# One tiling of the TensorE array throughout, the output product in one step, a band spread from one product, and another written-out order

## The chip, the cores and the metric

The kernel runs on one core of one Trainium2 chip. The metric is the time of the device in microseconds for one execution; of several runs the median is told.

## The reference

A causal convolution of seven taps, whose weights are a softmax over the taps for each of eight heads, and then a token mixer without a softmax. With B = 8, S = 4224, D = 192, H = 8 heads of 24 columns, KC = 7 taps and a hidden width DH = 64:

```python
w = softmax(weight, axis=-1)                     # [8, 7], with 1e-9 added to the sum
y[b, s, h, :] = sum_k w[h, k] * x_padded[b, s + k, h, :]    # six zero rows ahead of x
wq, wk = y @ w_q, y @ w_k                        # [B, S, 64]
W = (wq @ wk^T) / 8                              # [B, S, S]
mixed = W @ y
out = maximum(mixed, 0) @ w_out                  # float32
```

The S x S matrix is never formed: `mixed = wq @ (wk^T y) / 8`, and `wk^T y = w_k^T (y^T y)`, so that the mixer needs the Gram matrix `y^T y` (192 x 192) of a batch.

## The kernel before

**Tiling.** A batch's sequence is cut into 35 chunks of 122 tokens, each with six rows of the chunk before (`XW`, 128 partitions, cast to bf16 by the load). For what follows the transposition, it is cut into superblocks: four of 1024 tokens (two halves of 512, `nh` = 2) and one of 128 (`nh` = 1). The 192 columns of D are split as 128 (LO) and 64 (HI).

**Stages of a batch,** all on TensorE, each followed by an evacuation from PSUM on ScalarE (ACT) or VectorE (DVE):
- `conv` (L559): for each pair of heads, a product with a band matrix (`BAND`, 128 x 128 for each head), over nine (batch 0) or 18 chunks; evacuated to `Y` (L578).
- `tr_lo` (L598) and `tr_hi` (L633): transposes of the chunks' 128 and 64 columns, evacuated to `YTL` (L605) and `YTH` (L640). `tr_hi` writes two chunks to the two halves of the partitions.
- `wq` (L658, L662): the products with `w_q`, two halves of the superblock on the two halves of the array's columns; evacuated to `WQT` (L678).
- `gram` (L694): the Gram matrix, six chunks a step, three matmuls a chunk with 64 stationary columns each, in a PSUM bank of its own.
- `turn` (L720) and `m` (L737): from the Gram matrix the mixing weights `MSB` (64 rows twice, for the two halves) and `MBD` (two 64 x 64 blocks on the diagonal), evacuated on ACT (L755).
- `mix_lo` (L784) and `mix_hi` (L795) of the batch before: with `nh` = 2, `mix_lo` is two matmuls of 64 rows each, one on each half of the array's rows; then the maximum with zero to `RT` (L807 on ACT, L808 on DVE).
- the output product, two token groups of 128 in each half at a time: `fin_hi` (L835, 64 rows, on the halves of the array's rows) and `fin_lo` (L853, 128 rows), evacuated to `OUT` (L869) and stored by SP (L877).

So the array is used in four shapes (rows x columns): 128x128, 128x64 (two column halves), 64x128 (two row halves) and 64x64.

**Order.** Every operation is an `Op` with an estimate of its length. `Planner.plan` places them one by one: on each engine the operation with the lowest `vt` among those that its estimates call ready. An operation on TensorE with another shape (`mode`) than the last one pays `STAY` on its `vt` and `SWITCH` on its start. Operations for `both` go to the engine of ACT and DVE that is free first. PSUM has seven banks for this. What comes out is a fixed order for each engine, with semaphore waits. The `vt` of an operation is a formula of batch and position, plus `TURN[kind]`.

**Start.** The weights of the convolution come by one load (L338). `IDENT` is made by DVE and POOL (L345, L359). The softmax is a chain on DVE and ACT (L375 to L391). The band is made in two halves of four heads: for each tap one product on DVE (L412, `IDENTW` shifted times the tap's weight), summed on TensorE (L423) and copied by ACT (L433); the products lie in `OUT`. `conv` waits for its heads' half (`band_done`). The loads of `x` are issued on POOL (L479), in four groups for batch 0 and two for each later batch. `w_q`, `w_k` and `w_out` come by nine loads on SP (L503), issued when batch 0's third group has landed, with one semaphore; ten casts on ACT (L508) follow, and `wq`, `m` and the output product each wait for all of them.

## Time and profile before

| | |
|---|---|
| median of 3 runs | 177.99 us (177.98 to 179.53) |
| the profiled execution | 178.53 us |
| its span | 176.8 us |
| TensorE busy | 161.5 us, 2454 matmuls |
| DVE, ACT, POOL busy | 123.5, 122.6, 30.3 us |
| granted TensorE clock | 0.993 of full speed on average |

The span is the time from the first to the last instruction in the trace of one execution. PE is TensorE's matmuls and PEld its weight loads, which overlap with matmuls. In rows of the timeline the columns are start, duration, engine, line, operation, output and inputs, shape (stationary rows*columns, then the moving operand) and count; a merged row's duration is from the first start to the last end, and a matmul's own duration holds some 0.2 us of latency beside its streaming. In a row by stretches of time come the length, the busy time and number of instructions of the engine, the granted clock, the DMA share and GB/s.

### The profile page before, as it was taken

To read this page: it belongs to the slowest core of one execution; us is meant where nothing else is said; L and a number is where in the kernel's file an instruction comes from. 1 tells how busy PE (TensorE), PEld (TensorE's weight loads), DVE (VectorE), ACT (ScalarE), POOL (GpSimd) and SP (SyncE) were. 2 spreads that over 40 slices of the span, in tenths; PEclk is the share of its full clock that TensorE was granted. 3 is DMA by queue.
4 is the path that set the end of the run, shared out by engine and by line. 5 is a ranking of instruction groups with operands and counts; after the bars stand their busy time and mean duration, and the time that the engine had idled before them with its cause. 6 is when DMAs were issued, how large, how long until landed. Compare 5 with 4: busy or idle time off the path is not lost.

```text
span 176.8 us, 5567 instructions
## 1 busy us (share of the span) xinstructions
PE 161.5 (91%) x2454; PEld 112.3 (64%) x2454; DVE 123.5 (70%) x219; ACT 122.6 (69%) x209; POOL 30.3 (17%) x39
## 2 busy tenths in 40 slices
PE   0589849999999999999999999999999999999880
PEld 0249737676766777767686577666775778666440
DVE  5948776887567477677969866797658775887660
ACT  4054364957789996797768767587779846968870
POOL 7999731525230000000000000000000000000000
PEclk9999999999999999999999999999999999999997
DMA  3999999999999999999999995530844075556697
GB/s 30 160 190 189 197 197 190 190 194 191 212 318 312 249 230 333 248 307 232 286 283 233 322 266 203 231 151 4 352 185 180 28 296 226 233 237 279 257 398 287
DMA packets 48151, 40.26 MB, mean 228 GB/s; under 512 B 37632, under 2 KB 40960, under 8 KB 48128
## 3 DMA queue, kind: packets, MB, share of 16 engines
q0 software_dynamic: 36128, 13.61, 64.7%
q1 hardware_dynamic: 12000, 26.31, 39.9%
q8 instruction: 19, 0.31, 0.7%
q14 instruction: 4, 0.03, 0.0%
HBM read 27.56 MB, written 25.95 MB: 303 GB/s over the span
## 4 chain that ended last, share of the span: by engine, by line
PE 81%; DMA 8%; ACT 3%; SPq 2%; POOL 2%; issue 1%; POOLq 0%
PE ps L853 15%; PE ps L694 14%; PE ps L559 11%; PE ps L835 9%; PE ps L598 7%; DMA xw<-in_x_dram 5%; PE ps L633 5%; PE ps L784 5%; PE ps L658 5%; PE ps L795 5%; PE ps L662 4%; DMA whi<-in_moe_w_out_dram 3%; SPq L503 2%; POOL xw L479 1%; ACT out_sb L869 1%
## 5 line engine op out<-in xcount | busy, mean ns | idle before, releaser
L869 DVE COPY out_sb<-ps 128x768 f32<-128x768 f32 (+1 forms) x36 | 32.0, 891 | 25.4 <-PE ps L853 25.3
L807 ACT ACTIVATE rt<-ps 128x1024 bf16<-128x1024 f32 (+3 forms) x50 | 37.9, 770 | 14.0 <-PE ps L784 13.4
L578 ACT CAST y<-ps 122x864 bf16<-122x864 f32 (+3 forms) x49 | 36.9, 793 | 8.1 <-PE ps L559 7.6
L869 ACT COPY out_sb<-ps 128x768 f32<-128x768 f32 (+1 forms) x36 | 26.6, 746 | 10.7 <-PE ps L853 10.2
L694 PE MATMUL ps<-y 122*64 122x128 bf16 (+2 forms) x840 | 34.0, 222 | 0.0
L479 POOL DMA_DIRECT2D xw<-in_x_dram x34 | 29.9, 908 | 19.4 <-issue 18.6
L694 PEld LDWEIGHTS ps<-y 122*64 122x64 bf16 x840 | 28.0, 110 | 8.1 <-issue 7.6
L559 PE MATMUL ps<-xw,band 128*128 128x432 bf16 (+3 forms) x144 | 31.4, 323 | 0.8 <-ACT band L433 0.7
L853 PE MATMUL ps<-wol,rt 128*128 128x192 bf16 x264 | 30.5, 250 | 0.0
L853 PEld LDWEIGHTS ps<-wol,rt 128*128 128x128 bf16 x264 | 21.0, 116 | 7.8 <-issue 2.9
L578 DVE CAST y<-ps 122x816 bf16<-122x816 f32 (+3 forms) x23 | 20.6, 912 | 3.9 <-PE ps L559 3.6
L605 DVE COPY ytl<-ps 128x976 bf16<-128x976 bf16 (+1 forms) x40 | 23.0, 589 | 0.6 <-PE ps L598 0.2
L808 DVE TENSOR_SCALAR rt<-ps 128x512 bf16<-128x512 f32 (+3 forms) x30 | 20.1, 681 | 4.7 <-PE ps L784 2.7
L598 PE MATMUL ps<-ident,y 122*128 122x122 bf16 x280 | 20.5, 216 | 0.4 <-DVE y L578 0.4
L835 PE MATMUL ps<-woh,rt 64*128 64x192 bf16 x264 | 20.0, 250 | 1.0 <-ACT rt L807 0.7
L598 PEld LDWEIGHTS ps<-ident,y 122*128 122x128 bf16 x280 | 17.5, 97 | 4.4 <-ACT y L578 0.6
L640 DVE COPY yth<-ps 128x512 bf16<-128x512 bf16 (+1 forms) x40 | 14.9, 378 | 5.5 <-PE ps L633 5.1
L633 PE MATMUL ps<-ident,y 122*64 122x122 bf16 (+1 forms) x344 | 17.0, 217 | 0.0
L559 PEld LDWEIGHTS ps<-xw,band 128*128 128x128 bf16 x144 | 11.4, 97 | 7.8 <-issue 2.2
L658 PE MATMUL ps<-ytl,wql 128*64 128x512 bf16 (+1 forms) x72 | 14.6, 368 | 1.9 <-ACT woh L508 1.9
L835 PEld LDWEIGHTS ps<-woh,rt 64*128 64x128 bf16 x264 | 11.3, 114 | 7.9 <-ACT rt L807 1.5
L678 ACT CAST wqt<-ps 128x512 bf16<-128x512 f32 (+1 forms) x24 | 12.4, 532 | 5.2 <-PE ps L662 4.7
(63 smaller groups left out, 128.0 us busy)
## 6 DMA issues: line engine op xcount, KB each, us to landing
out_dram<-out_sb SPq DMA_DIRECT2D x28, 768.0 KB, 5.0
xw<-in_x_dram POOLq DMA_DIRECT2D x7, 816.0 KB, 30.3
xw<-in_x_dram POOLq DMA_DIRECT2D x7, 768.0 KB, 35.6
out_dram<-out_sb SPq DMA_DIRECT2D x8, 384.0 KB, 3.1
xw<-in_x_dram POOLq DMA_DIRECT2D x2, 432.0 KB, 8.3
out_dram<-out_sb SPq DMA_DIRECT2D x8, 96.0 KB, 3.6
xw<-in_x_dram POOLq DMA_DIRECT2D x1, 384.0 KB, 5.1
xw<-in_x_dram POOLq DMA_DIRECT2D x8, 45.8 KB, 23.8
```

Source lines behind the costliest of these rows:

```text
L479: lambda e, op, part=part: e.dma_start(*part),
L559: last = e.matmul(PS[:, o : o + n * GRP], BAND[:, h, :], XW[:, b, c0 : c0 + n, GRP * h : GRP * h + GRP], start=True, stop=True,)
L578: return e.copy(dst, src) if op.engine == "ACT" else e.tensor_copy(dst, src)
L598: last = e.transpose(ps[:, o : o + w], Y[0:w, yb, c, 0:LO], IDENT[0:w, 0:w])
L605: lambda e, op: e.tensor_copy(YTL[:, t0:t1], bank(mm_l.bank).bitcast(BF16)[:, 0:cols]),
L633: last = e.transpose(ps[64 * i : 64 * i + HI, o : o + w], Y[0:w, yb, c, LO:D], IDENT[0:w, 0:w])
L658: last = e.matmul(ps[64 * i : 64 * i + DH, 0:n], WQL[:, :], YTL[:, t0 + i * n : t0 + (i + 1) * n], start=True, stop=False)
L694: mm = e.matmul(bank(GB)[p : p + 64, o : o + z - r], Y[0:w, yb, c, r : r + 64], Y[0:w, yb, c, r:z], start=st, stop=end, skip_group_check=True,
L807: return e.activation(dst, src(), AF.Relu)
L835: last = e.matmul(bank(op.bank + a)[:, o : o + D], RT[64 * a : 64 * a + HI, slot, 2, i:n:nt], WOH[64 * a : 64 * a + HI, :], start=i == q, ...
L853: last = e.matmul(bank(fh.bank + a)[:, o : o + D], RT[:, slot, a, i:n:nt], WOL[:, :], start=False, stop=True, skip_group_check=True,)
L869: return e.copy(dst, src) if op.engine == "ACT" else e.tensor_copy(dst, src)
```

## The change

- All matmuls and transposes use stationary operands of 64 columns: what took the whole array becomes two matmuls or transposes on the column halves (`halves`, `turn_halves`).
- Where 64 rows were used, all 128 are, with zeros in the other half: `MSB` has one copy for each half of the superblock, the other half's rows zero; `WOH` is 128 x 384, with `w_out`'s last 64 rows once for each half of the superblock and zeros beside them. `mix_hi` becomes two matmuls.
- `fin_hi` and `fin_lo` become one operation, `fin`: for each token group one pair of 384 columns for both halves of the superblock, and for each half a pair of 192 columns added to it. Its banks are one for each token group, instead of one for each half.
- The band: rows of a matrix `TAPS` hold the weights of a tap at the place of a position within 16; a 0/1 matrix `STEPT`, made by a transpose, spreads it. Eight products (pairs of halves, 128 columns) give all eight heads, in two banks, copied by ACT and DVE. All convolutions wait for both copies. The softmax keeps the numerator of a partition's own tap by adding -10000 to the others ahead of the exponential.
- The three weights are issued once batch 0's second group has landed, each with a semaphore of its own, and their casts are waited for apart. There is one cast more.
- `vt` is a number from a table, one for each operation, instead of formula and `TURN`. With one shape, the planner never adds `SWITCH` after its first matmul.

```diff
-FULL, COL2, ROW2 = "128x128", "128x64", "64x128"
+TURNS = [
+    int(t) / 1000
+    for t in """
+-9360 -9860 -8870 -8880 -9260 -9760 -9760 -9160 -9060 -8960 -8910 -8910 -8860 -8850 -8840 -9360 -9310
+-9360 -9360 -9300 -9290 -9280 -8360 -8260 -8210 -8360 -8160 -7960 -7910 -7860 -7360 -7260 -6960 -7260
...
+COL2, ROW2 = "128x64", "64x128"
...
-    SWITCH = 95.0
-    STAY = 0.8
-    HOLD = 1
+    SWITCH = 145.0
+    STAY = 1.708
+    HOLD = 5
...
-        op.vt += TURN.get(kind, 0.0)
+        op.vt = TURNS[len(planner.ops)]
...
+    def halves(e, out, lhsT, rhs, **k):
+        e.matmul(out[0:64], lhsT[:, 0:64], rhs, **k)
+        return e.matmul(out[64:128], lhsT[:, 64:128], rhs, **k)
+
+    def turn_halves(e, out, in_, identity):
+        e.transpose(out[0:64], in_[:, 0:64], identity)
+        return e.transpose(out[64:128], in_[:, 64:128], identity)
...
+    zero_w = add("DVE", lambda e, op: e.memset(WQT[64:128, :, wq_cols[-2] :], 0.0), 150, vt=-8.51)
-    zero_b = add("DVE", lambda e, op: e.memset(BAND[:, :, CW:128], 0.0), 80, vt=-8.9)
+    zero_s = add("DVE", lambda e, op: e.memset(STEPT[:, :], 0.0), 150, vt=-8.9)
+    eps = add("DVE", lambda e, op: e.memset(WEX[:, 0, :, 7], 1e-9), 100, vt=-9.4)
+    zero_e = add("DVE", lambda e, op: e.memset(WEX[:, 1, :, 7], 0.0), 100, vt=-9.4)
...
+        add("DVE", lambda e, op: e.memset(MSB[:, :, :, :], 0.0), 300, vt=-8.49),
+    ]
+    zero_o = add("DVE", lambda e, op: e.memset(WOH[:, :, :], 0.0), 250, vt=-8.48)
...
-    identw = add(
+    step = add(
+        "DVE",
+        lambda e, op: e.tensor_copy(
+            STEP[:, :].rearrange("p (k i) -> p k i", i=16), bass.AP(IDENT[:, :].tensor, 0, [[128, 128], [1, 8], [1, 16]])
+        ),
+        200, needs=[ident], vt=-8.95)
+    turned = add(
+        "PE",
+        lambda e, op: turn_halves(e, bank(op.bank).bitcast(BF16)[:, 0:128], STEP[:, :], IDENT[:, :]),
+        60, needs=[step, ident], banks=1, vt=-9)
+    stept = add(
         "ACT",
...
+    by_tap = add(
...
+    other = add(
...
+    own = add(
...
+        def spread(e, op, q0=q0):
+            last = None
+            for q in range(q0, q0 + 4):
+                last = halves(
+                    e,
+                    bank(op.bank)[:, (q - q0) * 128 : (q - q0 + 1) * 128],
+                    STEPT[0:112, 112 - 16 * q : 240 - 16 * q],
+                    TAPS[0:112, :, :].rearrange("p i h -> p (i h)"),
...
+        bands.append(add(engine, band, 550, drains=fill, vt=-6.9))
...
-    load_c = add("SP", emit_weights, 5000, needs=load[0, 2], dma=("c", S_C, 16 * 9), tail=2500, vt=-3)
+        return add("SP", emit, 1700, needs=load[0, 1], dma=(name, semaphore(f"s_{name}"), 16 * 3), tail=4000, vt=vt)
+
+    load_q = gen_weight("wq", wq_t, DH, QS, -3.0)
+    load_k = gen_weight("wk", wk_t, DH, KS, -2.9)
+    load_o = gen_weight("wo", wo_t, D, OS, -2.8)
...
-        cast(WOH[:, :], WHI[:, OS]),
+        cast(WOH[0:HI, 0, :], WHI[0:HI, OS], load_o, [zero_o]),
+        cast(WOH[HI:128, 1, :], WHI[HI:128, OS], load_o, [zero_o]),
...
-                    last = e.matmul(
+                    last = halves(
+                        e,
                         PS[:, o : o + n * GRP],
                         BAND[:, h, :],
...
-                last = e.transpose(ps[:, o : o + w], Y[0:w, yb, c, 0:LO], IDENT[0:w, 0:w])
+                last = turn_halves(e, ps[:, o : o + w], Y[0:w, yb, c, 0:LO], IDENT[0:w, 0:w])
...
-            (lambda: MSB[:, mb, :], lambda: bank(mm.bank)[:, 0:LO], LO),
+            (lambda: MSB[0:64, mb, 0, :], lambda: bank(mm.bank)[0:64, 0:LO], LO),
+            (lambda: MSB[64:128, mb, 1, :], lambda: bank(mm.bank)[64:128, 0:LO], LO),
...
-                last = e.matmul(
-                    bank(op.bank + i)[:, 0:n],
-                    MSB[64 * i : 64 * i + DH, mb, :],
-                    WQT[64 * i : 64 * i + DH, wqb, q0 : q0 + n],
-                    start=True,
-                    stop=True,
-                )
+                last = halves(
+                    e, bank(op.bank + i)[:, 0:n], MSB[:, mb, i, :], WQT[:, wqb, q0 : q0 + n], start=True, stop=True
+                )
...
+            def fin(e, op, iq=iq, q=q):
                 last = None
                 for i in iq:
+                    o = bank(op.bank + i - q)
+                    last = halves(
+                        e,
+                        o[:, 0 : nh * D],
+                        RT[:, slot, 2, i:n:nt],
+                        WOH[:, 0:nh, :].rearrange("p t d -> p (t d)"),
...
                     for a in range(nh):
+                        last = halves(
+                            e,
+                            o[:, a * D : (a + 1) * D],
                             RT[:, slot, a, i:n:nt],
                             WOL[:, :],
...
+                src = src.rearrange("p i (t d) -> p i t d", t=nh)
+                dst = OUT[:, oslot, 0:nh, q : q + step, :].rearrange("p t i d -> p i t d")
```

## The prediction

> **What bounds the kernel now.** I read the page first, then TensorE's busy time by stretches, then the timeline of one piece of the steady part, then the first 30 us.

> ```profile
> span 176.8 us, 5567 instructions
> ...
> PE 161.5 (91%) x2454; PEld 112.3 (64%) x2454; DVE 123.5 (70%) x219; ACT 122.6 (69%) x209; POOL 30.3 (17%) x39
> ...
> PE   0589849999999999999999999999999999999880
> ```

> ```profile
> 10.00:20.00 10.00, 8.95 (x165) 1.00 1.57 189
> 20.00:30.00 10.00, 7.67 (x145) 1.00 1.56 198
> 30.00:150.00 120.00, 119.88 (x1906) 1.00 1.05 231
> ```

> TensorE is busy 119.88 of the 120 us from 30 to 150, at clock 1.00, and DVE and ACT only some 70% of the span. So the steady part is worth what TensorE's work is worth; the start and the tail are a matter of waits. But "busy" counts drains of the array too. What is streamed is read from starts:

> ```profile
> 66.63 0.38 PE L662 MATMUL ps<-yth,wqh 128*64 128x512 bf16 x2
> 66.84 0.38 PE L658 MATMUL ps<-ytl,wql 128*64 128x512 bf16 x2
> 67.06 0.38 PE L662 MATMUL ps<-yth,wqh 128*64 128x512 bf16 x2
> ...
> 70.86 0.43 PE L633 MATMUL ps<-ident,y 122*64 122x122 bf16 x9
> ...
> 71.80 0.52 PE L835 MATMUL ps<-woh,rt 64*128 64x192 bf16 x8
> 72.16 0.38 PE L784 MATMUL ps<-wqt,msb 64*128 64x512 bf16 x2
> 72.48 0.85 PE L853 MATMUL ps<-wol,rt 128*128 128x192 bf16 x8
> 73.16 0.38 PE L795 MATMUL ps<-wqt,mbd 128*128 128x512 bf16 x1
> 73.47 0.63 PE L694 MATMUL ps<-y 122*64 122x192 bf16 x15
> ```

> L658 and L662 are pairs on the two column halves; a pair of 512 columns starts every 0.216 us, no more than one full matmul of 512, so the halves stream side by side. Nine L633 take 0.43 us, eight steps and one latency of 0.217: 0.0266 us each, 0.053 for a pair of 122 columns. L853 (full array, 192 columns) steps by 0.0825. Where the shape changes there are holes: L784 (64 rows) streams 0.216, yet L853 (128 rows) starts 0.31 later; L795 streams 0.216, yet L694 (64 columns) starts 0.31 later. That is 0.094 us, and mostly about 0.025 more, because the second weight load after a change is not hidden: the start-to-start step behind it is 0.109 instead of 0.0825. I summed this over all matmul starts: 152 changes of shape; over the 108 stretches of one shape that begin between 30 and 150 us the time above streaming has a median of 0.121 us. So 152 x 0.121 = 18.4 us are lost to changes.

> Streaming, by counts times these steps: convolution L559 22.8, L598 14.8, L633 9.1, L658 and L662 14.3, L694 24.6 (0.088 a chunk), L720 and L737 1.8, L784 7.4, L795 7.4, L835 10.9, L853 21.8: 134.7 us, and 2.9 for the band, L423. TensorE's last start is at 172.1:
> 134.7 + 18.4 changes + 15.1 lost before 30 us (30 less 14.2 streamed and 0.7 of changes) + 1.9 other waits from 30 to 150 + 1.9 in the tail = 172.0. Another 4.7 (last evacuation and store) makes the span of 176.8.

> **The change, part by part. (1) One shape.** All 152 changes go: -18.4. Bounds: -14.3 by the drain alone (152 x 0.094), -18.4 by the median; I take the median, as the unhidden load is caused by the change.

> **(2) What it costs.** The row halves let two matmuls of 64 rows run together; zero rows do not. L784: a superblock of 1024 tokens had one pair of 512 columns (0.216) and now has two: +0.216 x 32 = +6.9. The output product: per two token groups it was two pairs of L835 (0.165) and four L853 (0.33), 0.495; now each group has a pair of 384 columns (384/2.4 + 2.5 = 162.5 ns) and two pairs of 192 (0.165), 0.655 for two. +0.160 x 64 = +10.2. The last 128 tokens of a batch cost the same. Together +17.2, so shape alone nets -1.2.

> **(3) Halves where the full array was.** Convolution, L598, L795, L853, L720, L737 become pairs. L658/L662 show a pair for the price of one, and both L662 of a pair read the same `yth` columns, as these halves do. For L598 a chunk goes from 0.0525 to the 0.053 of L633: +0.2. Not shown: halves that read `xw` in runs of 24, and 64-column weight loads with a stride, as in the output product. For the first, between nothing and a full second pass (22.8); I take nothing, from the nearest row, L662. For the second, loads of 0.116 (L853's) one after another would make a group 0.348 instead of 0.327: 0 to +2.7; I take 0, since L853 hides a strided load of twice the columns in 0.0825.

> [...]

> **(4) The start.**

> ```profile
> 9.29 0.57 ACT L433 CAST band<-ps 128x488 bf16<-128x488 f32 x1 [4.72 <-PE ps L423]
> ...
> 12.86 1.65 PE L559 MATMUL ps<-xw,band 128*128 128x216 bf16 x16 [0.69 <-ACT band L433]
> 13.19 0.33 SPq L503 DMA_DIRECT2D wlo<-in_moe_w_q_dram  x1
> ...
> 23.55 0.24 ACT L508 CAST wql<-wlo 128x64 bf16<-128x64 f32 x1 [1.59 <-DMA whi<-in_moe_w_out_dram]
> ...
> 26.24 0.41 PE L658 MATMUL ps<-ytl,wql 128*64 128x512 bf16 x2 [1.90 <-ACT woh L508]
> ```

> Four heads' band is ready for 10.0, the other four's at 12.86. Fourteen products of 0.33 us on DVE go. In their place DVE gets, between the identity (2.7) and the maximum (3.83 now), four small operations of about 0.2 and three more memsets: by the written order all eight memsets now stand ahead of the maximum, which moves to about 5.9. From there eight steps of 0.2 to 0.25 and their hops (2.4), eight half pairs on TensorE (0.45 to 0.9), one evacuation of 0.57 to 0.65 with two hops: all eight heads at about 10.0 (bounds 9.3 and 10.8). So the first convolution does not move; the second half of the heads gains 2.9, and L423 leaves TensorE.

> The weights: nine issues wait for batch 0's third load, landed at 13.17; now for the second, 10.81, and there are three semaphores. Three q issues end near 12.4; with the 5.0 us to landing of today 17.4, and three casts of 0.24 make L658 possible at about 18.1 instead of 26.24; k's casts end near 21, the output's near 22.5. Nothing else is queued on SP then (the first store comes after 47 us). Nine transfers of 0.29 MB come 2.4 us earlier between the `x` loads; at 190 GB/s that delays batch 1's first load (20.16) by 1.5 at most, while TensorE has work.

> Is there work? Loads land at 6.8, 10.8, 13.2, 15.1 (batch 0), 20.2, 25.3 (batch 1). From 10.0: batch 0 without L658/L662 is 8.9 us of streaming, these 1.8, then batch 1's first half 4.5 and batch 0's output side about 8: to beyond 30. I charge 1.5 us for the first evacuations' latency, so 11.5 are lost instead of 15.1: -3.6. Bounds: -5.1 (dense from 10.0) and 0 (each freed wait turns into another).

> **(5) The rest.** One more ACT copy of 0.2 to 0.28 us a batch in the chain to the mixing weights, hidden behind the previous batch's output work (exposed at start and end: 0.5, within the 1.5 and the tail). The output's evacuations have the same 768 columns. The written-out order may shrink the 1.9 + 1.9 of waits or, tuned to other durations than the chip's, raise them: 0 taken, -3.8 to +4.

> **Sum:** 134.7 + 17.2 + 11.5 + 3.8 + 0.2 + 4.7 = 172.1 for the span, -4.7. The profiled execution took 178.53 (1.7 around its span), the runs' median 177.99. Applied to the median: **173.3 us**.

> **Rivals. B, the order does more:** dense from 10.0 and few waits left: 134.7 + 17.4 + 10 + 4.7 = 166.8, as a time 168.0; half way there, 170. For it: five shapes no longer have to be gathered. Against: from 30 to 150 only 1.9 were left to gain.
> **E, the start gives nothing:** the k and output weights land late and hold the output side, so TensorE only rearranges its wait: 173.3 + 3.6 = 176.9, within 1% (what a measurement of this kernel can tell from no change).
> **D, slower: PSUM banks run out.** The output product holds two banks 0.16 longer (twice a superblock) and L784's two 0.22 longer: 4 x (0.64 + 0.43) = 4.3 bank-us a batch, and without drains the next product wants its bank 0.12 sooner, on some 19 occasions a batch with two banks, 4.6. 8.9 / 7 banks x 8 batches = 10.2 us if all of it becomes waiting: 183.5; half, 178.4. It decides once banks are held over some 95% of a batch. I estimate (evacuation of 0.6 to 1.0 plus stream and hops) 100 of 7 x 19 bank-us, 75%. For it: the tail, where TensorE does wait for `out_sb`. Against: in the steady part that releaser hardly appears.
> **C, slower: loads or reads of the halves pace TensorE.** If a half could not be reloaded before its load's whole record is over (110 ns, L633's load row), an L598 chunk would take 0.110: 280 x 0.057 = +16, 189; with convolution halves in turn, +22.8: 196. L633, with the same loads at 0.053 a pair, and L662 speak against. [...]

> **How the numbers follow.** Forecast 0.50 (own range 171 to 176), B 0.20, E 0.15, D 0.10, C 0.05. Faster by over 1% (under 176.2): forecast, B, and the better third of E less a little: 0.75. Slower (over 179.8): C and most of D: 0.12. The rest 0.13. The range runs from B's end, 168, to D's half way, 179.

> **What would show it.** TensorE's matmuls have 64 columns throughout; steps stay at 0.053 (122), 0.216 (512), 0.0825 (192) a pair, 0.18 for a convolution pair, and holes of 0.12 are gone. The output product shows 0.655 a piece. The first convolution starts at about 10, L658 near 18, and the 20 to 30 stretch is dense. Wrong if a pair's step is longer than one full matmul's, if TensorE's idle time names `out_sb` or `y` copies between 30 and 150, or if L658's successor still starts after 24.

## The result, and the profile after

The changed kernel takes **185.57 us** (median of 4 runs, 184.76 to 187.13); the kernel before took 178.3 in the same comparison. The ratio is **1.042** (95% interval 1.036 to 1.047): 4% slower, where 173.3 us was forecast and 168 to 179 given as the range.

The page of the changed kernel's profiled execution (184.76 us), first the span, the engines and TensorE's busy tenths, then the row of the DMA queue that the page calls `instruction`:

```profile
span 182.9 us, 7295 instructions
...
PE 160.7 (88%) x3314; PEld 135.9 (74%) x3314; DVE 123.8 (68%) x224; ACT 121.9 (67%) x209; POOL 30.3 (17%) x39
...
PE   0299589996999979949999999899999999999980
...
q8 instruction: 26, 0.43, 0.9%
```

860 matmuls and as many weight loads are new, yet TensorE is busy for about as long as before (161.5). The span is 6.1 us longer, and the row of tenths has dips that the row of before does not have. The last line counts packets, megabytes and share: 26 packets of 16 KB each (0.43 MB), called code packets below. The page of the kernel before has

```profile
q8 instruction: 19, 0.31, 0.7%
```

TensorE's busy time by stretches, columns as in the rows of before:

```profile
10.00:20.00 10.00, 7.92 (x197) 1.00 1.54 194
20.00:30.00 10.00, 9.25 (x173) 1.00 1.60 193
30.00:150.00 120.00, 113.84 (x2419) 1.00 1.01 214
```

The stretch from 30 to 150 us was full before (119.88 of 120). Now 6.2 us of it are idle, and in the first 30 us little was gained. The timeline shows what streaming costs (start, duration, engine, line, operation, output and inputs, shape, count):

```profile
63.93 0.33 PE L393 MATMUL ps<-woh,rt 128*64 128x384 bf16 x1
...
64.09 0.33 PE L393 MATMUL ps<-wol,rt 128*64 128x192 bf16 x2
...
64.26 0.33 PE L393 MATMUL ps<-woh,rt 128*64 128x384 bf16 x1
```

From one token group's first product to the next one's is 0.33 us, as forecast (0.655 for two). Pairs of 122 columns step by 0.053, of 192 by 0.0825, of 512 by 0.216. All pairs summed give 152.2 us of streaming (0.5 for the band besides), where 152.1 was forecast. So the time went elsewhere. The same timeline at the places where TensorE stood longest, the idle time before the row and what ended it in brackets:

```profile
20.21 0.37 PEld L794 LDWEIGHTS ps<-y 122*64 122x64 bf16 x11 [2.43 <-issue]
...
45.75 0.30 PE L733 MATMUL ps<-ident,y 122*64 122x122 bf16 x4 [1.66 <-issue]
...
81.50 0.36 DVE L967 COPY out_sb<-ps 128x192 f32<-128x192 f32 x1 [3.11 <-DMA out_dram<-out_sb]
81.91 0.11 PEld L393 LDWEIGHTS ps<-gsb,wkl 128*64 128x64 bf16 x1 [2.87 <-DVE out_sb L967]
```

Two kinds. In the first two rows (and at 65.65, 1.31 us from one start to the next) TensorE waits for nothing that the profile shows: "issue". In the last two, DVE stands on the evacuation of an output product, whose slot of `OUT` is not yet stored; the product `m` of the next batch needs a bank or a copy queued behind that evacuation, and TensorE stands with it.

The span by the prediction's terms (all rows but the last two add up to the start of the last matmul):

| us | before | forecast | after |
|---|---|---|---|
| streaming (band apart) | 134.7 | 152.1 | 152.2 |
| changes of shape | 18.4 | 0 | 0 |
| lost before 30 us | 15.1 | 11.5 | 14.8 |
| other waits, 30 to 150 us | 1.9 | 1.9 | 9.4 |
| tail | 1.9 | 1.9 | 1.3 |
| last evacuation and store | 4.7 | 4.7 | 5.2 |
| span | 176.8 | 172.1 | 182.9 |

### The profile page after: what moved, and what is told of

Read it like the earlier page. It is cut to its first block, busy times and chain, and to the rows that moved or that the text cites. A ratio compares the mean times of both kernels' runs of the same rounds, so it can differ in the third digit from the quotient of the medians.

```text
span 182.9 us, 7295 instructions
## 1 busy us (share of the span) xinstructions
PE 160.7 (88%) x3314; PEld 135.9 (74%) x3314; DVE 123.8 (68%) x224; ACT 121.9 (67%) x209; POOL 30.3 (17%) x39
## 4 chain that ended last, share of the span: by engine, by line
PE 72%; DMA 12%; DVE 6%; ACT 5%; issue 4%; DVEq 0%
PE ps L393 28%; PE ps L394 12%; DMA out_dram<-out_sb 12%; PE ps L794 11%; PE ps L733 5%; PE ps L894 4%; PE ps L397 4%; PE ps L398 3%; PE ps L758 3%; PE ps L762 3%; DVE out_sb L967 2%; ACT y L678 1%; ACT out_sb L967 1%; ACT msb L856 1%; ACT mbd L856 0%
## 5 line engine op out<-in xcount | busy, mean ns | idle before, releaser
L967 ACT COPY out_sb<-ps 128x768 f32<-128x768 f32 (+1 forms) x44 | 33.5, 766 | 21.1 <-PE ps L394 16.7
L393 PE MATMUL ps<-wol,rt 128*64 128x192 bf16 x264 | 43.7, 246 | 1.0 <-issue 1.0
L393 PE MATMUL ps<-woh,rt 128*64 128x384 bf16 (+1 forms) x136 | 44.2, 326 | 0.4 <-DVE rt L912 0.4
L394 PE MATMUL ps<-woh,rt 128*64 128x384 bf16 (+1 forms) x136 | 44.4, 327 | 0.0
L394 PE MATMUL ps<-wol,rt 128*64 128x192 bf16 x264 | 43.8, 246 | 0.0
L393 PEld LDWEIGHTS ps<-wol,rt 128*64 128x64 bf16 x264 | 35.9, 136 | 2.5 <-issue 1.3
L794 PE MATMUL ps<-y 122*64 122x128 bf16 (+3 forms) x840 | 34.0, 220 | 2.3 <-issue 2.3
L394 PEld LDWEIGHTS ps<-wol,rt 128*64 128x64 bf16 x264 | 36.0, 137 | 0.0
L794 PEld LDWEIGHTS ps<-y 122*64 122x64 bf16 (+1 forms) x840 | 31.6, 110 | 4.3 <-issue 2.4
L911 ACT ACTIVATE rt<-ps 128x1024 bf16<-128x1024 f32 (+2 forms) x41 | 31.6, 799 | 4.6 <-PE ps L394 4.3
L571 POOL DMA_DIRECT2D xw<-in_x_dram x34 | 29.9, 909 | 21.9 <-issue 21.1
L393 PE MATMUL ps<-xw,band 128*64 128x408 bf16 (+3 forms) x144 | 30.9, 336 | 1.9 <-DVE band L533 0.9
L394 PE MATMUL ps<-xw,band 128*64 128x408 bf16 (+3 forms) x144 | 31.0, 337 | 0.0
L912 DVE TENSOR_SCALAR rt<-ps 128x512 bf16<-128x512 f32 (+2 forms) x39 | 26.3, 696 | 5.3 <-PE ps L394 4.2
L397 PE MATMUL ps<-ident,y 122*64 122x122 bf16 (+1 forms) x280 | 20.7, 218 | 0.0
L393 PEld LDWEIGHTS ps<-woh,rt 128*64 128x64 bf16 x136 | 18.2, 134 | 3.0 <-ACT rt L911 1.7
L398 PE MATMUL ps<-ident,y 122*64 122x122 bf16 (+1 forms) x280 | 20.4, 218 | 0.0
## 6 DMA issues: line engine op xcount, KB each, us to landing
xw<-in_x_dram POOLq DMA_DIRECT2D x8, 45.8 KB, 25.3
```

The lines of the kernel that those rows point to most:

```text
L393: e.matmul(out[0:64], lhsT[:, 0:64], rhs, **k)
L394: return e.matmul(out[64:128], lhsT[:, 64:128], rhs, **k)
L397: e.transpose(out[0:64], in_[:, 0:64], identity)
L398: return e.transpose(out[64:128], in_[:, 64:128], identity)
L571: lambda e, op, part=part: e.dma_start(*part),
L794: mm = e.matmul(bank(GB)[p : p + 64, o : o + z - r], Y[0:w, yb, c, r : r + 64], Y[0:w, yb, c, r:z], start=st, stop=end, skip_group_check=True,
```

## The experiments

**The loads taken away.** The stands at "issue" all lie before 106 us, while `x` is still being loaded. Two kernels leave out most of that: batches 1 to 7 load one row instead of their chunks, and all batches convolve batch 0's data.

```diff
+        if b:
+            parts = [(XW[0:1, b, cs[0] + k, 0:64], bass.AP(x_t, base, [[D, 1], [1, 64]])) ...]
...
-                        XW[:, b, c0 : c0 + n, GRP * h : GRP * h + GRP],
+                        XW[:, 0, c0 : c0 + n, GRP * h : GRP * h + GRP],
```

In the kernel before:

> The kernel before, but the loads of x of batches 1 to 7 are cut to one row of 64 columns each, and every batch convolves batch 0's rows; the order of all instructions is kept. Theory L (in the changed kernel TensorE waits for its own code and for slots of the output buffer, both late because the loads of x keep the DMA engines busy until 106 us): the kernel before fetched code early enough and hardly waited for stores, so it gains little here, 1 to 2 us, near 177. Theory O (the written-out order is what loses): the same, 177.

In the changed one:

> The changed kernel with the same cut of the loads, its order kept. Theory L: the three holes of 2.5, 1.8 and 1.2 us at code fetches and the 2.6 us behind an output slot go, some 8 to 10 us: 175 to 177, no longer slower than the kernel before with the same cut. Theory O: the waits are in the order and the banks, and stay: 183 or more.

177.01 us (ratio to the kernel before 0.992, 0.989 to 0.995) and 177.95 (0.997, 0.993 to 1.000). The loads cost the kernel before 1.3 us and the changed kernel 7.6: 6.3 of the 7.3 us between the two kernels need the loads to be there, whichever waits they cause. The other 1.0 says that even so the change gains nothing over the kernel before; for the changed one, 175 to 177 was expected.

**The order alone.** The old formula and `TURN` in place of the table, nothing else, so that the order is planned anew:

> The changed kernel with the vt formulas and TURN of the kernel before (fin gets +0.035) in place of the table of numbers. Theory O: the table is what loses, so the formula comes to 178 or less. Theory L: as many instructions and the same loads, so similar holes: 183 to 189.

183.57 us (1.028, 1.021 to 1.034), 2.0 less than with the table. So the table is not the main thing that makes the change slow. Its waits for output slots do not come in this order, while stands at "issue" do, and shorter ones (1.3 us at 18.8, 0.3 and 0.4 near 83 and 89, 0.8 at 107.4). From 30 to 150 us TensorE is almost full:

```profile
30.00:150.00 120.00, 118.87 (x2486) 1.00 1.08 241
```

By the terms of the table above, this order loses 3.9 us there, 15.4 before 30 us (11.5 were forecast), 3.1 in the tail (1.9) and 6.2 in the last evacuation and store (4.7). What makes the last two longer was not tried.

**Five output slots.** `OUT` gets a fifth slot, all orders kept:

```diff
+    SLOTS = 5
...
-        slot, oslot = n_rt % NRT, n_out % NOUT
+        slot, oslot = n_rt % NRT, n_out % SLOTS
```

> The changed kernel with five slots of OUT instead of four, orders kept. If the waits for an output slot are worth what the trace shows at 79 us and near 110 to 125 us (2.6 and some 1.5), 181 to 183. If such a wait only takes the place of another one, 185.

182.17 us (1.022, 1.015 to 1.030): 3.4 less. The stand at 79.1 is gone. From 30 to 150 us TensorE is now busy for

```profile
30.00:150.00 120.00, 116.41 (x2495) 1.00 1.01 217
```

and what is left are stands at "issue": 1.4, 1.6 and 1.0 us at 45.3, 65.3 and 84.8, besides 2.1 at 17.9.

**The start.** The earlier and separate weight loads alone, in the kernel before:

```diff
-    load_c = add("SP", emit_weights, 5000, needs=load[0, 2], dma=("c", S_C, 16 * 9), tail=2500, vt=-3)
+        return add("SP", emit, 1700, needs=load[0, 1], dma=(name, semaphore(f"s_{name}"), 16 * 3), tail=4000, vt=vt)
```

> The kernel before with only the weights' part of the change: three semaphores, issued after batch 0's second group, casts waited for apart. The prediction's step: L658 starts near 18 instead of 26.2 and 2 to 3.6 us of the waits before 30 us go, 175. Rival: TensorE only does the same work in another order, or the transfers collide with the loads of x: 177.5 to 179.

178.49 us (1.001, 0.997 to 1.005): no difference in the whole. The wait for the weights gives way to a shorter one for batch 1's `x`, and from 20 to 30 us TensorE is busy for 8.85 us instead of 7.67:

```profile
21.07 1.27 PE L565 MATMUL ps<-xw,band 128*128 128x432 bf16 x6 [1.25 <-DMA xw<-in_x_dram]
```

```profile
20.00:30.00 10.00, 8.85 (x155) 1.00 1.60 192
```

Counted as in the prediction, 13.6 us are lost before 30 us instead of 15.1. But the order was planned anew for this kernel, and it has 163 changes of shape instead of 152; 1.6 us more are lost from 30 to 150 us. So the run shows a gain at the start and a loss behind it of the same size, and not that earlier weights gain nothing.

In the changed kernel the first convolutions also run at half pace. They begin at 9.2 us, but pairs of 216 columns start 0.18 apart until 12.1, where the streaming time is 0.093:

```profile
10.11 0.39 PE L393 MATMUL ps<-xw,band 128*64 128x216 bf16 x1
...
10.29 0.39 PE L393 MATMUL ps<-xw,band 128*64 128x216 bf16 x1
```

The column of the granted clock shows 1.00 for this stretch, but only because nothing is on record for it: the trace's records of the granted clock begin at 12.68 us here and at 10.53 in the kernel before, and a stretch without a record is shown as 1.00 (and so counted in the mean of 0.993 given above). In the kernel before too, matmuls take about twice their streaming time just before the first record. There the band's products L423 kept TensorE busy from 6.2 us on and took most of this on themselves (0.41 us a step for 488 columns up to 9.5 us, 0.20 to 0.21 from 10.6 on); the convolutions at 12.86 (16 of 216 columns in 1.65 us) had full pace. So eight pairs of 512 columns on the identity were put ahead of the band in the changed kernel:

> The changed kernel with eight pairs of 512 columns on the identity between 3.9 and 7.3 us, where TensorE idles, into the Gram matrix's bank. If the convolutions from 9.3 to 12 us step by 0.174 instead of 0.093 because TensorE idled before, they step by 0.093 and 0.5 to 1.2 us go, of which the loads of x may take back a part: 184 to 185. Rival (they wait for the evacuations): no change.

184.72 us (1.036, 1.028 to 1.045, against 1.042): no clear change. The added pairs themselves ran at half pace (0.43 apart), but then eight pairs of the convolution, from 8.84 us on, went at full pace. Then TensorE waited for the next load of `x`, and the following eight were 0.18 apart again, this time with the granted clock on record:

```profile
8.84 0.25 PE L395 MATMUL ps<-xw,band 128*64 128x216 bf16 x1 [0.88 <-DVE band L545]
...
8.93 0.25 PE L395 MATMUL ps<-xw,band 128*64 128x216 bf16 x1
...
10.39 0.39 PE L395 MATMUL ps<-xw,band 128*64 128x216 bf16 x1 [0.62 <-DMA xw<-in_x_dram]
...
10.57 0.39 PE L395 MATMUL ps<-xw,band 128*64 128x216 bf16 x1
```

```profile
6.95:10.37 3.42, 1.57 (x32) 1.00 1.49 173
10.37:13.78 3.41, 3.39 (x54) 0.50 1.59 189
```

So with work put ahead the full pace came sooner (at 8.84 us, where without it the half pace lasts until 12.1), and a stretch in which TensorE was busy for less than half of the time (1.57 of 3.42 us) was followed by 3.41 us at half the clock. What a start without that pause would be worth was not tried. Such a stretch of 3.41 us at 0.50 also followed some long stands: of 2.1 us in the kernel with five slots (from 20.1 us on), of 2.5 in the paced one (86.6) and of 2.3 with halves throughout (22.9), but none in the changed kernel's own profile. TensorE loses up to 1.7 us by one, as an estimate from its length and clock.

**The loads paced.** Those of batch b+1 wait for the first convolution of batch b:

```diff
+        for gi in range(len(groups_of(b + 1))):
+            for x in load[b + 1, gi]:
+                x.needs.append(mm)
```

> The changed kernel with the loads of x for batch b+1 held back until the first convolution of batch b (for b from 1), orders kept, so that the DMA engines rest between batches. Theory L (code and output slots late behind the loads): the holes near 44, 64 and 79 us go or shrink, those before 25 us stay: 179 to 182. Rival (only the sum of the traffic counts, or the loads now come late): 185 or more.

187.11 us (1.046, 1.037 to 1.055): not better. The stands stayed, and new ones came later (2.5 us at 83.0, 0.75 at 138.1), since the loads now last to 133 us. But the trace tells when code comes late, as the next part shows.

**What the trace says of "issue".** Number TensorE's records (weight loads, matmuls and the few of its waits) by start, from 0. The stands at "issue" of the changed kernel begin at records 449, 1473 and 2241, and those of other kernels at 449, 705, 1217, 1729, 2497, 3009, 3265, 4033 and others: all 193 above a multiple of 256, and 26 packets on q8 for 6685 records are one packet for each 257 (before: 19 for 4947, one for each 260). With eight pairs added at the start, the stands remained at 449 and 1473, that is at other operations. And all 41 stands of over 0.25 us at such records that the nine kernels with column halves and full loads show before 106 us end 2.2 to 2.6 us after a code packet starts. The reading that fits all this is that TensorE has no instructions there; no row of the trace says so directly. For each block of 256, three times can be read: when the block before was begun, when the packet of code starts ("lag" after that), and how long TensorE takes for 256 when nothing holds it. For the blocks that end before 106 us:

| kernel | shortest, median time of 256 | median lag | stood at boundaries |
|---|---|---|---|
| before | 6.3, 8.0 us | 3.1 us | 0 |
| before, loads cut | 6.3, 8.0 | 0.4 | 0 |
| after | 4.1, 6.2 | 3.8 | 5.8 us at 4 |
| after, loads cut | 4.1, 6.2 | 0.8 | 1.1 at 3 |
| after, five slots | 4.1, 6.2 | 3.9 | 6.1 at 4 |
| after, order by formula | 4.5, 6.1 | 3.8 | 2.3 at 5 |

So, as an estimate from the median lag of the changed kernel and the middle of the 2.2 to 2.6 us, a block must last about 3.8 + 2.4 = 6.2 us while `x` is loaded. Before, every block does; after, half of them don't. The order by formula has as many instructions, and its stands are less than half as long: its shortest block lasts 4.5 us, and most are close to 6.2. One stand does not fit: with the loads cut, 0.8 of the 1.1 us stand at 18.1 us and end 4.4 us after the packet starts; why is open. In the paced run the lag was 0.2 to 1.9 us at the three fetches with at most 50 packets of `x` in the 3 us before, and 3.1 to 5.0 at the nine with 745 or more (one with 563 had 1.5): in this run the packet starts later when loads are under way. Behind 106 us this is less clean: one fetch in that run had 4.1 us with 23 packets.

**Attempts to add code only.** No-ops in the kernel before did not reach the program (178.26 us, with the same 4947 records of TensorE as before) and told nothing. Instead of them, waits on a semaphore that was long met:

```diff
+    def pad(e):
+        for _ in range(3):
+            e.wait_ge(S_W, 16)
```

> The kernel before, with three more waits that are already met (on the semaphore that the first load set, long past) ahead of each convolution, each transpose to the low rows and each matmul of the output product: TensorE's instructions go from 4947 to some 6030, so its code from 0.31 to some 0.39 MB, about as much as the change's 6685 instructions and 0.43 MB. No matmul, shape, order or load is changed. Theory K (holes come from more code that is fetched while x is loaded): holes of 1 to 2.5 us on TensorE that end on no wait, each a little after a fetch of code begins, one to four of them before 106 us, so 2 to 7 us more than the same kernel with cut loads shows, about 181 to 186 us. Rival (the holes come from something else in the change, such as its many short matmul pairs or its order): no such holes, and the time is the one before plus what the waits cost themselves, the same surplus as with cut loads.

> The same additional waits in the kernel before whose loads of x for batches 1 to 7 are cut to one row (all batches convolve batch 0). It gives what the waits cost by themselves: without them this kernel took 177.01 us. Theory K: no holes at code fetches after the first 20 us, so the difference between the run with loads and this one grows from 1.3 us (178.3 to 177.01 without the waits) to 3 to 8 us. Rival: the difference stays 1 to 2 us.

214.74 us (1.200, 1.191 to 1.208) and 214.72 (1.198, 1.189 to 1.207): no difference between full and cut loads, and no stands of over 0.25 us. As a test of the cause it failed: 1085 instructions more cost 36 us, 34 ns each, so TensorE took 5.4 us or more, mostly 6 to 9, for 256 of its instructions, waits included, and could not outrun its code. What it does show is that more code by itself, at this pace, makes no stands.

**Better orders and a mix.** Two candidates from a search over the constants of the order:

> The kernel before with another set of constants for its order alone (TURN, STAY 0.786, SWITCH 121): no tiling, load or buffer is changed, 164 changes of shape in place of 152. If order is what leaves time on the table, some of the 1.9 us of waits from 30 to 150 us and of the 15.1 us before 30 us goes: 174 to 177 us. Rival: the waits that decide (code, output slots, the first loads) are not in the order's estimates, and it comes out within 1% of 178.3 or slower.

> The kernel before with column halves for the convolution, the transposes, the products after the Gram matrix, mix_hi and fin_lo, while mix_lo and fin_hi stay on the row halves as before (none of the 6.9 and 10.2 us that the change pays for zero rows), and constants of the order for this: 129 changes of shape in place of 152, so at 0.121 us each 2.8 us less. TensorE's instructions grow nearly as much as in the change. If halves cost nothing by themselves: 175 to 176 us. Theory K (more code, fetched late while x is loaded): holes of 1 to 2.5 us as in the change take the gain back, 178 to 183 us.

183.8 us (1.027, 1.020 to 1.035) and 181.44 (1.013, 1.006 to 1.019). The first one's estimates do not hold on the chip: TensorE stands for 2.5 us at 23.4 (weights) and 2.3 at 96.0 (an output slot), and not at code boundaries. So a poor order alone can cost 5 us. The mix, with all its changes of shape, has 5.8 us of stands at eight boundaries before 106 us, its blocks taking 5.7 us in the median.

**Halves late, early, throughout.** Three kernels keep the order of before operation for operation and use column halves for the whole-array operations in one part of the run (`vt` of 5 is passed at about 100 us). The cut shows the late one; the early one has `op.vt < 5.0`, and the third splits always:

```diff
+    def split(op):
+        return op.vt >= 5.0
...
-                    last = e.matmul(
+                    last = halves(
+                        e, op,
```

> The kernel before, its order kept operation for operation, with column halves for the whole-array operations only where vt is 5 or more, that is from about 100 us on, when nearly all of x is loaded. 143 changes of shape in place of 152, so 1.1 us less. Theory D (TensorE runs dry when 256 of its instructions pass in less than the 3 to 4 us that a code fetch starts late while x is loaded, plus the 2.2 to 2.6 us until it can be used): after 106 us a fetch starts 0 to 2.5 us after the boundary, so 256 instructions may pass in 5 us, and no hole ending at a record 193 modulo 256 is over 0.5 us: 176.5 to 177.7 us. Theory A (more code costs, wherever it stands) or halves cost by themselves: holes in the second half of the run, 178.5 us or more.

> The same with column halves only where vt is below 5, that is until about 100 us, while x is loaded; 142 changes of shape, so 1.2 us less by these alone, and about the same additional code as the run with late halves. Theory D: blocks of 256 instructions pass in 5 to 6 us there, and at several of the records 449, 705, 961 and so on up to 100 us TensorE stands 0.5 to 2 us, 3 to 6 us in all: 179.5 to 183 us. Theory A: as much as the run with late halves, within 1 us.

> The same with column halves throughout (row halves kept), in the order of before: 113 to 119 changes of shape in place of 152, so 4.0 to 4.7 us less. This is the tiling of the change alone, without zero rows, one-step output product, band, weights or order. Theory D: the holes of the run with early halves come back, 3 to 6 us, so 177 to 181 us. If halves in themselves cost nothing and no holes come: 173.6 to 174.3 us.

Late: 178.85 us (1.006, 1.004 to 1.008). Early: 183.62 (1.030, 1.026 to 1.034), a little over what was expected. Throughout: 179.49 (1.008, 1.005 to 1.011). TensorE's busy time from 30 to 100 us, late first, then early:

```profile
30.00:100.00 70.00, 69.91 (x1109) 1.00 1.40 257
```

```profile
30.00:100.00 70.00, 67.45 (x1408) 1.00 1.41 252
```

The two have nearly as much code (22 and 23 packets). With early halves TensorE stands at eight boundaries for 6.6 us, the first of them

```profile
22.56 0.24 PE L345 MATMUL ps<-ident,y 122*64 122x122 bf16 x1 [2.30 <-issue]
```

and in the late kernel at none, although its blocks then mostly take 5.4 to 7 us: the lag is down to 0.1 to 2.4 us once the loads are done. So the cause of these stands is density of instructions under loads, not the amount of code and not the halves as such. The expected size was missed for the late ones: the last matmul starts 0.9 us earlier than before (171.2, 172.1), as nine changes fewer should give, but the time after it is 5.9 us instead of 4.7, and the run is 0.6% slower. That last part (evacuation and store) was 4.4 to 6.4 us in these three kernels, and why was not tried. Throughout, TensorE stands for 5.6 us at nine boundaries; 33 to 39 fewer changes of shape are worth 4.0 to 4.7.

**Thinner code in the changed kernel.** With five slots, same order, only the transposes to the low rows back on the whole array:

```diff
-                last = turn_halves(e, ps[:, o : o + w], Y[0:w, yb, c, 0:LO], IDENT[0:w, 0:w])
+                last = e.transpose(ps[:, o : o + w], Y[0:w, yb, c, 0:LO], IDENT[0:w, 0:w])
```

> The changed kernel with five output slots (182.17 us when it ran), its order kept operation for operation, but with the transposes of the 128 low columns on the whole array again: 280 matmuls and as many weight loads less, 68 changes of shape more, which at 0.121 us each cost 8.2 us. Theory D: the blocks with transposes take longer, and of the 6.1 us that TensorE stood at records 449, 1473, 2241 and 3009 at most 2 us are left: 182.17 + 8.2 - 4 to 6 = 184 to 186.5 us. If the holes come from something else in the change they stay, and it takes 189.5 to 191 us.

184.06 us (1.035, 1.032 to 1.038), 1.9 more than with halves for 68 changes of shape that cost 8.2 by the prediction's price. 1.1 us of stands at boundaries are left of 6.1, and the stretch is full again:

```profile
30.00:150.00 120.00, 119.79 (x2247) 1.00 1.02 218
```

"Full" means here that the holes at changes of shape (0.094 us without streaming, and mostly 0.025 more, in the rows of before) count as busy. No version that computes everything was faster than the kernel before.

## Why the prediction was wrong

**Right: what streams.** Parts (1) to (3) came out within 0.1 us: the 152 changes are gone, zero rows and the one-step output product cost 17.2, halves cost nothing in streaming, neither those that read `xw` in runs of 24 nor those with strided weight loads (137 ns for a load's record, no effect on the step). Rival C does not hold. Two 64-column loads, whose records last 110 ns each, and two transposes pass in 0.053 us a chunk, the step of the whole-array transposes of before, so the loads do not pace them. The prediction's 162.5 ns for 384 columns is an estimate: 384/2.4 + 2.5 lies on the line through the steps of before for 192 columns (0.0825) and 512 (0.216). The runs show the token group as a whole, 0.33 us.

**Failed: "other waits 1.9", part (5).** The halves were costed by matmul time alone. That they double the instructions for the same time was seen nowhere in the sum. Of the 7.5 us too little, 3.0 are stands at code boundaries (1.8 and 1.2 beyond streaming), 3.8 are waits for output slots (2.6 at 79.1, 0.8 and 0.4 later), and 0.3 is a wait for the mixing weights at 121.8, which stays with five slots. Idle time that names `out_sb` between 30 and 150 us was one of the prediction's own signs of being wrong. The waits for slots lie within the +4 that part (5) gave for an order made for other durations, and five slots take 3.4 us off. As for the stands at boundaries, nothing in the trace of before showed a stand, but its q8 row and its instruction count did show 260 instructions a packet (4947 records, 19 packets), and the packets' starts a median lag of 3.1 us.

**Failed: the start, part (4).** 3.6 us were to be gained, 0.3 were. The early band came even sooner than its bounds (9.2; 10.0 forecast, 9.3 to 10.8), and the casts of the q weights begin at 17.3; but their first product, forecast for about 18.1, came at 21.1. The first boundary costs 2.4 us at 17.7, and half pace until 12.7 costs 1.6 us (16 pairs at 0.087 too long, five of 122 columns at 0.04). Without these, lost time would be 10.8, close to the 11.5. Part (4) counted it as a gain that the band's products leave TensorE; it did not see that these had run through the half pace, which now falls on the convolutions. Earlier weights alone are worth about 1.5 us before 30 us in the kernel before, which its newly planned order lost again.

**The rivals.** E's time (176.9) does not hold for the change, and its mechanism, a start that gives nothing, was not shown: the weights alone gained something there. D named the right symptom, TensorE held by the output side, but not the resource: slots of `OUT` and not PSUM banks, 3.8 us; that it decides once banks are held over 95% of a batch was the author's estimate, which no run tested. B has nothing for it. The range missed since none of the rivals was about the supply of instructions.

**How far it closes.** The span is 10.8 us over the forecast. Stands at code boundaries (5.4), output slots (3.8), the half pace at the start (1.6) and the mixing weights (0.3) make 11.1; the rest are small differences both ways. Five slots give 3.4 us. Of the remaining 3.9 us to the kernel before (182.17 against 178.3), the 6.1 us at code boundaries are more than enough. That removing them would give all 6.1 was not shown: with loads cut, where 1.1 is left, the changed kernel still takes 177.95. With the order by formula, where stands at boundaries are about 3 us, it takes 183.57, so the order's own waits matter as well. How long the half pace at the start lasts differs between executions (until 12.7 us in the changed kernel's trace, and up to 15.2 in other traces where convolutions begin at 9.2), and what decides it was not tried.

## What to carry to other kernels

Splitting matmuls into column halves was free in streaming here (0.053 us for a transposed chunk either way) and not free in instructions (860 matmuls and 860 weight loads more): count the engine's instructions for each microsecond, and compare the time of 256 of them with the time that a code packet takes in that stage, here about 6.2 us while `x` was loaded, by the estimate above. A stand that ends on "issue" at record numbers with one remainder modulo 256 is, by the reading above, missing code, and in the paced run the lag of its packet went with the loads under way (0.2 to 1.9 us with few packets of `x`, 3.1 to 5.0 at the nine fetches with 745 or more). That speaks for thinner code where loads run, and the dense form later: early halves had 6.6 us of stands at boundaries, late ones none, though the late kernel was not faster than the one before either (1.006). When TensorE gets rid of its holes at changes of shape, look at what the output side can store, slots included, before crediting the gain: a fifth slot gave 3.4 us. Read the pace at the start from the steps of the matmuls: the clock column shows 1.00 where nothing is on record, here until 12.68 us.
